# The second expert layer's first product for batches 1 to 3: seven quarter products in place of eight

## The chip, the cores and the metric

The kernel runs on one core of one Trainium2 chip. The metric is the device time of one execution in microseconds. Engines are named as the profile names them: PE is the matrix engine (its weight loads are PEld), DVE the vector engine, ACT the scalar engine, POOL the GpSimd engine, SP the engine whose queue issues the transfers here.

## The reference

Attention over q, k and v of 4 batches by 8 heads by 1152 positions of 64, with pairs of query rows averaged, gives 2304 rows x of 512 columns, 576 rows for each batch. A first expert layer maps them back to 2304 by 512. The change is in the second:

```python
def _moe2_ref(x, w1, w2, w3, w_out) -> np.ndarray:
    h = np.maximum(np.maximum(x @ w1, x @ w2), x @ w3)
    return (h @ w_out).astype(np.float32)
```

Here x is 2304 by 512, each of w1, w2 and w3 is 512 by 768, w_out is 768 by 512.

## The kernel before, in words

Every number is carried as a pair of 16-bit floats, a high part and the rest, so each 32-bit product is three matmuls: high by high, high by rest, rest by high. The kernel has three stages that run into each other: attention, the first expert layer (`up_step`, `down_step`, whose result goes to DRAM as `y_d` for each batch, L680), and the second expert layer. While the first layer finishes, `w_m_steps` (L756) loads w1 to w3, scales them and splits them into `wm` (the two parts, three matrices, four 128-row blocks `kt`, 768 columns).

The second layer goes batch by batch. `load_y(b)` (L806) makes the batch's scale, loads `yf` from `y_d` and splits it into `yh`: the high part on POOL (L825), the rest on DVE (L827). `h2_group(b, half, ff, yh)` (L847) makes one 128 by 288 block of h: for each of the three matrices, 12 matmuls of 288 columns (four `kt` by three) into one PSUM bank (L854), so 36 matmuls a group and 12 groups a batch (two halves of the rows, six blocks `ff` of the 768 columns). ACT copies the first bank to `mx` (L858), DVE takes the maximum with the second and third (L859, L860), ACT writes the high part of h (L862) and DVE the rest (L863). The six banks of `ps2` hold two groups.

`w_o_steps` (L780) loads w_out in six pieces: `to_f32` (L240 to L254) turns each from 64-bit words into 32-bit floats with one ACT and four DVE instructions (L245, L247, L248, L251, L253), then it is scaled and split (L237, L238 of `split_rows`). `out_tiles(b)` (L866) makes four 128-row tiles of the output with 18 matmuls of 512 columns each (L871), an ACT copy with the scale (L874) and a store (L876). The last 64 rows of two batches share a tile in `out_rest` (L879): 36 matmuls into the two halves of a bank (L885), two ACT copies (L889), two stores.

The order of the first two stages is written out in a table. In the second layer the tile framework orders each engine's queue: each engine's instructions stand in a fixed queue, made ahead of the run by taking, as the engine comes free in the framework's own reckoning, a ready instruction that comes early in the program. Batch 0's groups are interleaved with the pieces of `w_o_steps`; from batch 1 on the tiles of the batch before come between the groups. The pool `wrw` has three buffers under the tag `raw`; the pieces of w1 to w3 and of w_out and the `yf` tiles take turns in them.

## Time and profile before

| what | us |
|---|---|
| median of 3 runs | 1154.99 |
| lowest and highest | 1154.86, 1156.99 |
| the profiled execution's own time | 1153.67 |
| its span, from the first instruction to the last | 1151.9 |
| PE busy in the span | 1056.3 |
| DVE busy in the span | 851.4 |

The profile is of one execution on the one core. Times in rows are counted from the start of the span; between the span and the execution's own time lie 1.8 us. An instruction's own duration includes its start-up and the way of its last result, so two in a row on one engine overlap in the rows: what one costs in a full queue is read from the distance of their starts. Granted clock (PEclk) is a share of PE's full 2.4 GHz: 1.00 is that, 0.50 is 1.2 GHz.

### The profile page before, as it was taken

To read this page: it belongs to the slowest core of one execution; us is meant where nothing else is said; L and a number is where in the kernel's file an instruction comes from. 1 tells how busy PE (TensorE), PEld (TensorE's weight loads), DVE (VectorE), ACT (ScalarE), POOL (GpSimd) and SP (SyncE) were. 2 spreads that over 40 slices of the span, in tenths; PEclk is the share of its full clock that TensorE was granted. 3 is DMA by queue.
4 is the path that set the end of the run, shared out by engine and by line. 5 is a ranking of instruction groups with operands and counts; after the bars stand their busy time and mean duration, and the time that the engine had idled before them with its cause. 6 is when DMAs were issued, how large, how long until landed. Compare 5 with 4: busy or idle time off the path is not lost.

```text
span 1151.9 us, 26593 instructions
## 1 busy us (share of the span) xinstructions
PE 1056.3 (92%) x11061; PEld 870.0 (76%) x11061; DVE 851.4 (74%) x1440; ACT 737.9 (64%) x1301; POOL 149.5 (13%) x160
## 2 busy tenths in 40 slices
PE   1578988899999999999998999997799999999998
PEld 1356865778888888888887888886797877767674
DVE  6999898789989899888897888877987532422220
ACT  6688887877888878888886888875564211112111
POOL 2301011221001222111122010000200110100000
PEclk9898998899999999999999999998899999999999
DMA  9962353378667898665688656557335110000001
GB/s 330 221 199 87 101 129 83 92 160 156 117 118 143 174 176 172 129 118 118 142 170 163 116 114 105 104 91 212 115 129 164 42 40 19 11 19 20 19 19 46
DMA packets 273753, 134.90 MB, mean 117 GB/s; under 512 B 229088, under 2 KB 256736, under 8 KB 272608
## 3 DMA queue, kind: packets, MB, share of 16 engines
q1 hardware_dynamic: 273632, 133.20, 51.0%
q8 instruction: 87, 1.43, 0.5%
q14 instruction: 34, 0.28, 0.1%
HBM read 62.39 MB, written 9.44 MB: 62 GB/s over the span
## 4 chain that ended last, share of the span: by engine, by line
PE 44%; DVE 3%; DMA 1%; ACT 1%; issue 1%; SPq 0%; POOL 0%; ACTq 0%; POOLq 0%; DVEq 0%
PE p L854 18%; PE py L673 7%; PE ph L648 6%; PE po L871 5%; PE sc L472 3%; PE av L581 3%; PE tr L536 1%; PE por L885 1%; DVE t L654 1%; DMA vn<-in_v_dram 0%; DVE st_m L247 0%; DMA raw_o<-in_moe_w_out_dram 0%; DVE st_m L253 0%; DVE st_m L251 0%; DMA kn<-in_k_dram 0%
## 5 line engine op out<-in xcount | busy, mean ns | idle before, releaser
L648 PE MATMUL ph<-xh,win 128*128 128x192 f16 x2304 | 209.0, 251 | 9.7 <-POOL xh L358 7.1
L854 PE MATMUL p<-yh,wm 128*128 128x288 f16 x1728 | 214.8, 286 | 1.6 <-DVE yh L827 0.8
L487 DVE TENSOR_REDUCE st<-sc 128x1 f32<-128x1152 f32 x144 | 194.7, 1352 | 20.9 <-PE sc L472 20.3
L648 PEld LDWEIGHTS <-win 128*128 128x128 f16 x2304 | 197.8, 100 | 14.3 <-issue 9.9
L673 PE MATMUL py<-g,wou 128*128 128x192 f16 x2304 | 199.1, 247 | 6.0 <-ACT g L657 5.7
L854 PEld LDWEIGHTS <-wm 128*128 128x128 f16 x1728 | 169.0, 98 | 47.0 <-issue 2.5
L673 PEld LDWEIGHTS <-wou 128*128 128x128 f16 x2304 | 189.7, 98 | 13.8 <-issue 12.7
L494 ACT ACTIVATE pf<-sc,st,esc 128x1152 f32<-128x1152 f32 x144 | 188.6, 1310 | 14.2 <-DVE st L489 6.6
L472 PE MATMUL sc<-kst,qst 128*64 128x512 f16 (+3 forms) x1152 | 169.0, 332 | 16.8 <-DMA kst<-kpre 7.2
L472 PEld LDWEIGHTS <-qst 128*64 128x64 f16 (+1 forms) x1152 | 80.6, 105 | 77.0 <-issue 27.3
L536 PE MATMUL tr<-ident,pf 128*128 128x128 f32 x648 | 89.4, 288 | 18.1 <-ACT pf L494 17.5
L862 ACT ACTIVATE h<-mx 128x288 f16<-128x288 f32 x48 | 21.2, 442 | 128.8 <-DVE mx L860 128.8
L560 DVE TENSOR_TENSOR hl<-pf,hl 128x1152 f16<-128x1152 f32 x72 | 98.3, 1366 | 3.7 <-ACT hl L558 1.7
L859 DVE TENSOR_TENSOR mx<-p,mx 128x288 f32<-128x288 f32 x48 | 21.8, 456 | 105.1 <-PE p L854 104.6
L536 PEld LDWEIGHTS tr<-ident,pf 128*128 128x128 f32 x648 | 75.2, 148 | 27.4 <-ACT pf L494 20.7
L581 PE MATMUL av<-pt,vhl 128*64 128x192 f16 x1944 | 87.1, 247 | 0.0
L558 ACT ACTIVATE hl<-pf 128x1152 f16<-128x1152 f32 x72 | 83.5, 1160 | 1.5
L581 PEld LDWEIGHTS <-vhl 128*64 128x64 f16 x1944 | 79.3, 110 | 6.8 <-issue 6.4
L657 ACT ACTIVATE g<-t,dgs 128x384 f16<-128x384 f32 x96 | 58.0, 609 | 15.3 <-DVE t L655 14.8
L652 ACT ACTIVATE t<-ph,Uv 128x384 f32<-128x384 f32 x96 | 55.0, 574 | 15.7 <-PE ph L648 14.7
L871 PE MATMUL po<-wo,h 128*128 128x512 f16 x288 | 64.3, 379 | 0.0
L659 DVE SCALAR_TENSOR_TENSOR g<-t,dgs,g 128x384 f16<-128x384 f32 x96 | 62.0, 648 | 2.7 <-ACT g L657 2.4
(178 smaller groups left out, 1264.9 us busy)
## 6 DMA issues: line engine op xcount, KB each, us to landing
vn<-in_v_dram SPq DMA_DIRECT2D x16, 576.0 KB, 4.9
kn<-in_k_dram SPq DMA_DIRECT2D x16, 576.0 KB, 4.4
raw_m<-in_moe_w_dram SPq DMA_DIRECT2D x12, 768.0 KB, 4.3
raw_in<-in_moe_w_in_dram SPq DMA_DIRECT2D x8, 1024.0 KB, 6.6
qn<-in_q_dram SPq DMA_DIRECT2D x24, 256.0 KB, 4.0
raw_ou<-in_moe_w_out_dram SPq DMA_DIRECT2D x10, 512.0 KB, 4.1
qst<-qst SPq DMA_DIRECT2D x48, 96.0 KB, 2.5
y_d<-ys SPq DMA_DIRECT2D x48, 96.0 KB, 2.0
```

Source lines behind the costliest of these rows:

```text
L472: nc.tensor.matmul(sc[m0:m1, n0:n1], qst[b, i, p][who][:, var, m0:m1], ks[:, h, n0:n1], start=(var == 0), stop=(var == 1))
L487: nc.vector.tensor_reduce(out=m, in_=sc, axis=AX.X, op=ALU.max, negate=True)
L494: nc.scalar.activation(out=pf, in_=sc, func=AF.Exp, bias=nb, scale=e, accum_out=sums[b, i, p][:, who:who + 1])
L536: nc.tensor.transpose(tr[:, c * P:(c + 1) * P], pf[:, c * P:(c + 1) * P], ident)
L558: nc.scalar.activation(out=hl[:, 0], in_=pf, func=AF.Copy)
L560: nc.vector.tensor_tensor(out=hl[:, 1], in0=pf, in1=hl[:, 0], op=ALU.subtract)
L581: nc.tensor.matmul(acc[64 * h:64 * h + 64], vhl[b, p][:, vi, h, c, :], pt[:, h, pi * KT + c, :], start=(c == 0 and e == 0), stop=(c == KT ...
L648: nc.tensor.matmul(ph[:, a], win[:, wi, kt, ff * P:(ff + 1) * P], x[:, xi, kt], start=(kt == 0 and e == 0), stop=(kt == KD - 1 and e == 2))
L659: nc.vector.scalar_tensor_tensor(out=g[:, 1, fs, :], in0=t2, scalar=gs, in1=g[:, 0, fs, :], op0=ALU.mult, op1=ALU.subtract)
L673: nc.tensor.matmul(py, wou[:, ff // 2, wi, ff % 2, m * P:(m + 1) * P], g[:, gi, ff, :], start=(ff == 0 and e == 0), stop=(ff == NF - 1 and ...
L854: nc.tensor.matmul(ph[:, :NB2], wm[:, wi, i, kt, ff * P:(ff + 1) * P], yh[:, yi, kt, n0:n0 + NB2], start=(kt == 0 and e == 0), stop=(kt == ...
L871: nc.tensor.matmul(po, h2t[b][:, hi, ff, t * P:(t + 1) * P], wo[:, wi, ff, :], start=(ff == 0 and e == 0), stop=(ff == NF2 - 1 and e == 2))
```

## The change

For batches 1 to 3 the product of a batch's 576 rows with each of the three matrices is cut into quarters (two halves of the 512 inner columns, two halves of rows, two halves of the 768 columns) and made by Winograd's form of Strassen's scheme. `weight_sums(j)` forms three sums of weight quarters for each of three column blocks j (two additions on POOL, the rest on DVE, the split on ACT and DVE), `sum_over(j)` a fourth, written over a quarter that batch 0 needs no more (three passes on POOL, one on ACT and DVE each). `load_parts(b)` takes the place of `load_y(b)` and forms the sums of the rows (four passes on DVE, and a split into seven pairs on ACT and DVE). `unit(b, j, i)` makes the four blocks of h for one j and one matrix i with seven products of six matmuls; the sums of products are made by accumulating in a PSUM bank and by additions on DVE. Batch 0 keeps `h2_group`; `plan` says which steps follow each of its 12 groups. PE's order is now the program's. `load_y(0)` splits on ACT and DVE. Even batches keep 640 rows of h (their 576 and 64 of the next batch's), so each output tile has 128 rows; the last tile is made in two halves of 256 columns. Output tiles use the two banks of `psg`. Powers of two in the scales are changed to leave room for the sums (left out below, as is the removed code that stands in the functions above).

```diff
         for h in range(2):
-            st = ep.tile([P, 3, DM], F32, tag="wst", bufs=2, name=f"st_o{h}")
+            st = ws[:, 1 + h].rearrange("p a b c d e -> p (a b c d e)").bitcast(F32)[:, :3 * DM]
+            st = st.rearrange("p (a b) -> p a b", a=3)
...
-    def load_y(b):
+    def y_scale(b):
...
+    def load_y(b):
+        y_scale(b)
         yh = wst.tile([P, 2, KD, SQ], F16, tag="st", name=f"yh{b}")
         for k2 in range(KD // 2):
             yf = wrw.tile([P, 2, SQ], F32, tag="raw", name=f"yf{b}_{k2}")
             nc.sync.dma_start(out=yf, in_=y_d[b][:, 2 * k2:2 * k2 + 2])
             for a in range(2):
                 kt = 2 * k2 + a
-                nc.gpsimd.tensor_scalar(out=yh[:, 0, kt, :], in0=yf[:, a], scalar1=ys[:, kt:kt + 1], scalar2=1.0,
-                                        op0=ALU.mult, op1=ALU.mult)
-                nc.vector.scalar_tensor_tensor(out=yh[:, 1, kt, :], in0=yf[:, a], scalar=ys[:, kt:kt + 1],
-                                               in1=yh[:, 0, kt, :], op0=ALU.mult, op1=ALU.subtract)
+                split_rows(yh[:, 0, kt, :], yh[:, 1, kt, :], yf[:, a], ysc[b][:, kt:kt + 1])
         return yh
...
+    HM = NF2 // 2
+    def store_h2(b, ff, half, m):
+        n0 = half * NB2
+        if b % 2 == 0:
+            cuts = [(h2t[b], n0, 0, NB2)]
+        elif half == 0:
+            cuts = [(h2t[b - 1], SQ, 0, 64), (h2t[b], 0, 64, NB2)]
+        else:
+            cuts = [(h2t[b], n0 - 64, 0, NB2)]
+        for hh, d0, c0, c1 in cuts:
+            hi, lo = (hh[:, e, ff, d0:d0 + c1 - c0] for e in range(2))
+            nc.scalar.activation(out=hi, in_=m[:, c0:c1], func=AF.Copy, scale=2.0 ** -16)
+            nc.vector.scalar_tensor_tensor(out=lo, in0=m[:, c0:c1], scalar=2.0 ** -16, in1=hi, op0=ALU.mult,
+                                           op1=ALU.subtract)
     def h2_group(b, half, ff, yh):
...
+        store_h2(b, ff, half, m)
+    def quarter(e, m, k, j):
+        return wm[:, e, :, 2 * k:2 * k + 2, (j + HM * m) * P:(j + HM * m + 1) * P]
+    def pass_(eng, out_, a, b_, op):
+        eng.tensor_tensor(out=out_, in0=a, in1=b_, op=op)
+    q_ = lambda e, m, k, j: quarter(e, m - 1, k - 1, j)
+    def weight_sums(j):
+        t1 = wrw.tile([P, 2, 3, 2, P], F32, tag="raw", name=f"ws{j}")
+        t2 = wrw.tile([P, 2, 3, 2, P], F32, tag="raw", name=f"wt{j}")
+        s1, s2, s4 = t1[:, 0], t1[:, 1], t2[:, 0]
+        def parts(n, x):
+            hi, lo = ws[:, j, n, 0], ws[:, j, n, 1]
+            nc.scalar.activation(out=hi, in_=x, func=AF.Copy)
+            pass_(nc.vector, lo, x, hi, ALU.subtract)
+        pass_(nc.gpsimd, s1, q_(0, 2, 1, j), q_(0, 2, 2, j), ALU.add)
+        pass_(nc.vector, s1, s1, q_(1, 2, 1, j), ALU.add)
+        pass_(nc.vector, s1, s1, q_(1, 2, 2, j), ALU.add)
+        parts(0, s1)
+        yield
+        pass_(nc.vector, s2, s1, q_(0, 1, 1, j), ALU.subtract)
+        pass_(nc.vector, s2, s2, q_(1, 1, 1, j), ALU.subtract)
+        parts(1, s2)
+        yield
+        pass_(nc.gpsimd, s4, q_(0, 1, 2, j), s2, ALU.subtract)
+        pass_(nc.vector, s4, s4, q_(1, 1, 2, j), ALU.add)
+        parts(2, s4)
+        yield
+    def sum_over(j):
+        s3 = wrw.tile([P, 3, 2, P], F32, tag="raw", name=f"wv{j}")
+        hi, lo = quarter(0, 1, 0, j), quarter(1, 1, 0, j)
+        pass_(nc.gpsimd, s3, q_(0, 1, 1, j), hi, ALU.subtract)
+        pass_(nc.gpsimd, s3, s3, q_(1, 1, 1, j), ALU.add)
+        pass_(nc.gpsimd, s3, s3, lo, ALU.subtract)
+        nc.scalar.activation(out=hi, in_=s3, func=AF.Copy)
+        pass_(nc.vector, lo, s3, hi, ALU.subtract)
+    def load_parts(b):
+        yf = []
+        for k2 in range(2):
+            f = wrw.tile([P, 2, SQ], F32, tag="raw", name=f"yf{b}_{k2}")
+            nc.sync.dma_start(out=f, in_=y_d[b][:, 2 * k2:2 * k2 + 2])
+            yf.append(f)
+        scale_y(b)
+        yield
+        for k2 in range(2):
+            for a in range(2):
+                nc.scalar.activation(out=yf[k2][:, a], in_=yf[k2][:, a], func=AF.Copy,
+                                     scale=ysc[b][:, 2 * k2 + a:2 * k2 + a + 1])
+        rw = yp.tile([P, 3, 2, 2, NB2], F16, tag="rw", name=f"yr{b}")
+        ts = wst.tile([P, 4, 2, 2, NB2], F16, tag="st", name=f"yt{b}")
+        b11, b12 = yf[0][:, :, :NB2], yf[0][:, :, NB2:]
+        b21, b22 = yf[1][:, :, :NB2], yf[1][:, :, NB2:]
+        def parts(d, x):
+            nc.scalar.activation(out=d[:, 0], in_=x, func=AF.Copy)
+            pass_(nc.vector, d[:, 1], x, d[:, 0], ALU.subtract)
+        parts(rw[:, 0], b11)
+        yield
+        pass_(nc.vector, b11, b12, b11, ALU.subtract)
+        parts(ts[:, 0], b11)
+        yield
+        parts(rw[:, 2], b22)
+        pass_(nc.vector, b12, b22, b12, ALU.subtract)
+        yield
+        pass_(nc.vector, b22, b22, b11, ALU.subtract)
+        parts(ts[:, 1], b22)
+        yield
+        parts(rw[:, 1], b21)
+        parts(ts[:, 2], b12)
+        yield
+        pass_(nc.vector, b21, b21, b22, ALU.subtract)
+        parts(ts[:, 3], b21)
+        both_y[b] = rw, ts
+        yield
+    both_y = {}
+    def product(ps, w, x, first, last):
+        for kt in range(2):
+            for e, (wi, xi) in enumerate(((0, 0), (0, 1), (1, 0))):
+                nc.tensor.matmul(ps[:, :NB2], w(wi, kt), x[:, xi, kt], start=(first and kt == 0 and e == 0),
+                                 stop=(kt == 1 and e == 2), skip_group_check=not first)
+    tops = {}
+    def unit(b, j, i):
+        rw, ts = both_y[b]
+        raw_w = lambda m, k: lambda e, kt: wm[:, e, i, 2 * k - 2 + kt, (j + HM * m - HM) * P:(j + HM * m - HM + 1) * P]
+        sum_w = lambda n: lambda e, kt: ws[:, j, n, e, i, kt]
+        key = f"{b}_{j}_{i}"
+        bank = lambda x: ps2.tile([P, 512], F32, tag="p2", name=f"p{x}_{key}")
+        def copied(ps, tag):
+            c = ep.tile([P, NB2], F32, tag=tag, bufs=2, name=f"{tag}_{key}")
+            nc.scalar.activation(out=c, in_=ps[:, :NB2], func=AF.Copy)
+            return c
+        def block(q_, ps, other):
+            ff, half = j + HM * (q_ // 2), q_ % 2
+            if i == 0:
+                m = tops[b, j, q_] = ep.tile([P, NB2], F32, tag="mx", name=f"mx{b}_{ff}_{half}")
+                if other is None:
+                    nc.scalar.activation(out=m, in_=ps[:, :NB2], func=AF.Copy)
+                else:
+                    nc.vector.tensor_tensor(out=m, in0=ps[:, :NB2], in1=other, op=ALU.add)
+                return
+            m, x = tops[b, j, q_], ps[:, :NB2]
+            if other is not None:
+                nc.vector.tensor_tensor(out=other, in0=ps[:, :NB2], in1=other, op=ALU.add)
+                x = other
+            nc.vector.tensor_tensor(out=m, in0=x, in1=m, op=ALU.max)
+            if i == 2:
+                store_h2(b, ff, half, m)
+        a = bank("a")
+        product(a, raw_w(1, 1), rw[:, 0], True, False)
+        s1 = copied(a, "s1")
+        b_ = bank("b")
+        product(b_, sum_w(0), ts[:, 0], True, False)
+        s5 = copied(b_, "s5")
+        yield
+        product(a, sum_w(1), ts[:, 1], False, False)
+        s2 = copied(a, "s2")
+        c = bank("c")
+        product(c, raw_w(1, 2), rw[:, 1], True, True)
+        block(0, c, s1)
+        product(b_, sum_w(2), rw[:, 2], False, True)
+        block(1, b_, s2)
+        product(a, raw_w(2, 1), ts[:, 2], False, False)
+        block(3, a, s5)
+        yield
+        product(a, raw_w(2, 2), ts[:, 3], False, True)
+        block(2, a, None)
+        yield
+    def out_tile(b, t, last=False):
         hh = h2t[b]
+        r0 = b * SQ + t * P + 64 * (b % 2)
+        g = gd2["mid", b] if t == 4 else gd2[b]
+        cuts = ((0, DM // 2), (DM // 2, DM)) if last else ((0, DM),)
+        for c0, c1 in cuts:
+            po = psg.tile([P, 512], F32, tag="g1", name=f"po{b}_{t}_{c0}")[:, :c1 - c0]
+            order_ = [ff for j in range(HM) for ff in (j, j + HM)] if b else list(range(NF2))
+            for n, ff in enumerate(order_):
                 for e, (hi, wi) in enumerate(((0, 0), (0, 1), (1, 0))):
+                    nc.tensor.matmul(po, hh[:, hi, ff, t * P:(t + 1) * P], wo[:, wi, ff, c0:c1],
+                                     start=(n == 0 and e == 0), stop=(n == NF2 - 1 and e == 2))
+            os = ep.tile([P, DM], F32, tag="os", bufs=3, name=f"os{b}_{t}_{c0}")[:, :c1 - c0]
+            nc.scalar.activation(out=os, in_=po, func=AF.Copy, scale=g)
+            nc.sync.dma_start(out=out[r0:r0 + P, c0:c1], in_=os)
     dn.close()
...
+    hp = ctx.enter_context(tc.tile_pool(name="hp", bufs=2))
+    wsp = ctx.enter_context(tc.tile_pool(name="wsp", bufs=1))
+    yp = ctx.enter_context(tc.tile_pool(name="yp", bufs=2))
+    ep = ctx.enter_context(tc.tile_pool(name="ep", bufs=6))
+    ws = wsp.tile([P, HM, 3, 2, 3, 2, P], F16, name="ws")
+    room_h = lambda b: hp.tile([P, 2, NF2, SQ + 64], F16, tag="h2", name=f"h2_{b}")
+    def second():
+        out_scale(0)
+        yield from load_parts(1)
+        out_scale(1)
+    w_o, y1, sums_of = w_o_steps(), second(), [weight_sums(j) for j in range(HM)]
+    plan = {0: (w_o, 2), 1: (w_o, 2), 2: (w_o, 2), 3: (sums_of[0], 2), 4: (sums_of[0], 2), 5: (w_o, 9), 6: (y1, 4),
+            7: (y1, 9), 8: (sums_of[1], 2), 9: (sums_of[1], 2), 10: (sums_of[2], 2), 11: (sums_of[2], 2)}
+    with tc.manual_schedule(engines={mybir.EngineType.PE}):
+        h2t[0] = room_h(0)
+        for g in range(2 * NF2):
+            h2_group(0, g // NF2, g % NF2, first_h)
+            run(*plan[g])
+            if g >= NF2 + HM:
+                sum_over(g - NF2 - HM)
+        todo = [(0, t) for t in range(4)]
+        prev = None
+        for b in range(1, B):
+            h2t[b] = room_h(b)
+            slots = (1, 3, 5, 7) if len(todo) == 4 else (0, 2, 4, 6, 8)
+            nxt = load_parts(b + 1) if b + 1 < B else iter(())
+            for n, (j, i) in enumerate((j, i) for j in range(HM) for i in range(3)):
+                u = unit(b, j, i)
+                run(u, 1)
+                if prev is not None:
+                    run(prev, 1)
+                run(u, 1)
+                prev = u
+                if n >= 1:
+                    next(nxt, None)
+                if n == 8:
+                    for _ in nxt:
+                        pass
+                    if b + 1 < B:
+                        out_scale(b + 1)
+                if n in slots:
+                    out_tile(*todo.pop(0))
+            assert not todo
+            if b % 2 == 1:
+                todo = [(b - 1, 4)]
+            todo += [(b, t) for t in range(4)]
+        run(prev, 1)
+        for n, (b, t) in enumerate(todo):
+            out_tile(b, t, n == len(todo) - 1)
 _INS = ['q', 'k', 'v', 'moe_w_in', 'moe_w_out', 'moe2_w1', 'moe2_w2', 'moe2_w3', 'moe2_w_out']
```

## Rows read from the trace of the kernel before

**Rows 1.** Stretches of batches 0 to 3: PE, PEld, DVE, ACT, POOL, clock, DMA, GB/s.

```profile
862.90:884.00 21.10, 19.78 (x160) 15.52 (x160) 19.05 (x38) 9.95 (x24) 3.58 (x3) 1.00 0.57 174
884.00:917.70 33.70, 33.70 (x280) 27.01 (x278) 20.06 (x43) 10.88 (x20) 3.90 (x4) 1.00 0.18 54
917.70:1127.50 209.80, 209.80 (x1555) 150.16 (x1553) 58.24 (x126) 40.31 (x86) 7.79 (x8) 1.00 0.07 23
```

**Rows 2.** Timeline of PE in the second layer (start, length, instructions merged).

```profile
908.88 13.39 PE L854 MATMUL p<-yh,wm 128*128 128x288 f16 x108
...
1050.17 17.81 PE L854 MATMUL p<-yh,wm 128*128 128x288 f16 x144
1067.82 4.05 PE L871 MATMUL po<-wo,h 128*128 128x512 f16 x18
1071.71 8.98 PE L854 MATMUL p<-yh,wm 128*128 128x288 f16 x72
...
1143.10 4.08 PE L885 MATMUL por<-wo,h 128*64 128x512 f16 x36
```

**Rows 3.** Timeline of ACT at the end.

```profile
1147.26 1.39 ACT L889 ACTIVATE osr<-por,gk 64x512 f32<-64x512 f32 x2 [3.32 <-PE por L885]
```

**Rows 4.** Timeline of DVE, instructions of 768 columns.

```profile
808.80 0.95 DVE L253 SCALAR_TENSOR_TENSOR st_m<-raw_m,st_m 128x768 uint32<-128x768 uint32 x1
809.67 0.95 DVE L251 SCALAR_TENSOR_TENSOR st_m<-raw_m,st_m 128x768 uint32<-128x768 uint32 x1
```

**Rows 5.** Timeline of DVE in batch 0 of the second layer.

```profile
873.35 0.82 DVE L859 TENSOR_TENSOR mx<-p,mx 128x288 f32<-128x288 f32 x2
...
884.29 0.69 DVE L253 SCALAR_TENSOR_TENSOR st_o<-raw_o,st_o 128x512 uint32<-128x512 uint32 x1
...
895.95 0.15 DVE L176 TENSOR_SCALAR U_o<-sum_o 128x1 uint32<-128x1 uint32 x1
...
898.13 3.55 DVE L238 SCALAR_TENSOR_TENSOR wo<-st_o,s_o,wo 128x1536 f16<-128x1536 f32 x2 [1.13 <-ACT wo L237]
```

**Rows 6.** One tile's instructions, yh on DVE (min, median, max ns; first, last start).

```profile
L827 DVE SCALAR_TENSOR_TENSOR yh<-yf,ysc,yh x16: 802/1212/1295, 862.8 to 997.5; 128x576 f16<-128x576 f32 x16
```

**Rows 7.** Groups of POOL instructions (count, busy us, mean ns, idle before).

```profile
L433 POOL TENSOR_TENSOR qn<-qn 128x384 f32<-128x384 f32 x24 | 28.8, 1201 | 109.6 <-DMA qn<-in_q_dram 82.3 <-DVE st L489 7.1 <-DVE xf L595 6.8
...
L775 POOL TENSOR_TENSOR wm<-st_m,wm 128x2304 f16<-128x2304 f32 x1 | 4.7, 4728 | 0.1
```

**Rows 8.** Timeline of DVE around three POOL instructions.

```profile
286.62 2.19 DVE L560 TENSOR_TENSOR hl<-pf,hl 128x1152 f16<-128x1152 f32 x1
...
378.66 1.36 DVE L546 TENSOR_TENSOR pt<-tr,pt 128x1152 f16<-128x1152 f32 x1
...
404.85 1.36 DVE L560 TENSOR_TENSOR hl<-pf,hl 128x1152 f16<-128x1152 f32 x1
```

**Rows 9.** Timeline of POOL in the same three places.

```profile
286.59 1.00 POOL L433 TENSOR_TENSOR qn<-qn 128x384 f32<-128x384 f32 x1 [0.32 <-DMA qn<-in_q_dram]
...
378.32 1.23 POOL L358 TENSOR_SCALAR kpre<-kn,sb 128x1152 f16<-128x1152 f32 x1 [0.26 <-DVE sqq L176]
...
405.09 1.57 POOL L358 TENSOR_SCALAR qpre<-qn,sqq 128x384 f16<-128x384 f32 x1 [3.87 <-ACT ys L677]
```

**Rows 10.** Timeline of DVE while batch 1's rows are split.

```profile
912.66 0.44 DVE L859 TENSOR_TENSOR mx<-p,mx 128x288 f32<-128x288 f32 x1
913.02 2.14 DVE L827 SCALAR_TENSOR_TENSOR yh<-yf,ysc,yh 128x576 f16<-128x576 f32 x2
915.09 0.45 DVE L860 TENSOR_TENSOR mx<-p,mx 128x288 f32<-128x288 f32 x1
```

**Rows 11.** Stretches around a gap on PE, columns as in rows 1.

```profile
816.00:820.00 4.00, 0.00 (x0) 0.00 (x0) 4.00 (x5) 0.54 (x2) 1.40 (x1) 0.83 0.18 33
820.00:824.00 4.00, 3.88 (x25) 3.56 (x25) 2.54 (x6) 2.82 (x5) 0.00 (x0) 0.50 0.73 236
824.00:828.00 4.00, 4.00 (x42) 3.88 (x41) 3.65 (x9) 4.00 (x8) 0.00 (x0) 0.81 0.40 155
```

More of the change, by code (lines that the diff above doesn't have):

```diff
@@ L813, in load_y @@
         nc.vector.tensor_reduce(out=zs, in_=z, axis=AX.XY, op=ALU.add)
[L814 removed]
+        root_scale(hu, c, all_add(zs, 1, f"y{b}"), 1, 4.0)
         hus[b] = hu
[L817 to L818 removed]
+        ysc[b] = late.tile([P, KD], F32, tag="ys", name=f"ysc{b}")
+        nc.vector.tensor_scalar(out=ysc[b], in0=u_m, scalar1=c, scalar2=None, op0=ALU.mult)
+    def load_y(b):
+        y_scale(b)
         yh = wst.tile([P, 2, KD, SQ], F16, tag="st", name=f"yh{b}")
@@ L879, in out_rest @@
-    def out_rest(b0):
-        os = ep.tile([P, DM], F32, tag="os", bufs=3, name=f"osr{b0}")
-        po = ps2.tile([P, 512], F32, tag="p2", name=f"por{b0}")
-        for ff in range(NF2):
-            for e, (hi, wi) in enumerate(((0, 0), (0, 1), (1, 0))):
-                for j in range(2):
-                    nc.tensor.matmul(po[64 * j:64 * j + 64, :], h2t[b0 + j][:, hi, ff, 4 * P:SQ], wo[:, wi, ff, :],
-                                     start=(ff == 0 and e == 0), stop=(ff == NF2 - 1 and e == 2))
-        for j in range(2):
-            rows = slice(64 * j, 64 * j + 64)
-            nc.scalar.activation(out=os[rows], in_=po[rows], func=AF.Copy, scale=gd2[b0 + j][rows])
-            r0 = (b0 + j) * SQ + 4 * P
-            nc.sync.dma_start(out=out[r0:r0 + 64, :], in_=os[rows])
-        yield
@@ L894, in body @@
-    nxt = first_y[0]
-    dn.close()
-    hp = ctx.enter_context(tc.tile_pool(name="hp", bufs=3))
-    ep = ctx.enter_context(tc.tile_pool(name="ep", bufs=3))
-    wgen = w_o_steps()
-    pend = None
-    for b in range(B):
-        yh = nxt
-        h2t[b] = hp.tile([P, 2, NF2, SQ], F16, tag="h2", name=f"h2_{b}")
-        for half in range(2):
-            for ff in range(NF2):
-                h2_group(b, half, ff, yh)
-                if b == 0:
-                    next(wgen, None)
-                    if half == 1 and ff == 3:
-                        run(wgen)
-                        out_scale(0)
-                        nxt = load_y(1)
-                        out_scale(1)
-                elif b + 1 < B and half == 0 and ff == 0:
-                    nxt = load_y(b + 1)
-                    out_scale(b + 1)
-                if pend is not None and ff % 2 == 1:
-                    if next(pend, "end") == "end":
-                        pend = None
-        if pend is not None:
-            run(pend)
-        if b % 2 == 0:
-            pend = out_tiles(b)
-        else:
-            def both(b=b):
-                yield from out_tiles(b)
-                yield from out_rest(b - 1)
-            pend = both()
```

36 lines of the change are left out of this document (14 added, 22 removed).

## The prediction

> **What bounds the kernel now.** I read the busy time by stretches first. From 884.0 to 1127.5 us PE is busy in every microsecond at full clock [rows 1]; DVE is busy 20.06 of 33.70 us in the second half of batch 0 and 58.24 of 209.80 us in batches 1 to 3. So in batches 1 to 3 a matmul that goes takes its whole spacing off the time, and DVE has room for more; in batch 0 DVE has some 13 us left, and it is there that most of the new preparation is put. The timeline of PE then gives the spacing [rows 2], that of DVE the prices of its instructions [rows 4 to 6], POOL's groups those of its own [rows 7], and a pair of timelines what the two do to each other [rows 8, 9].
>
> **What PE loses.** A unit has seven products of six matmuls, 42, where eight would have 48. There are 3 batches by 3 column blocks by 3 matrices, 27 units: 162 matmuls fewer. 144 of them take from 1050.17 to 1067.82 [rows 2], 0.1226 us each: **19.9 us off**. A tile of 18 takes 3.89 us (1067.82 to 1071.71), a tile of `out_rest`, 4.08 recorded against 4.05, the same; 18 before, 18 after: nothing. At the end two copies of 0.69 us stand in a row behind the last matmul [rows 3]; after it one of 256 columns: between 0.7 (a copy as long as now) and 1.0 (half as long) goes, I take **0.9 off**.
>
> **What the added instructions cost.** On DVE one over 768 columns costs 0.87 us, the distance of two starts [rows 4]; one over 288 costs 0.37 (two in 0.82, the second 0.45 long) [rows 5]; one over 576 takes 0.80 undisturbed [rows 6], less 0.08 of overlap 0.72; a half of w_out's split 1.77, a scale instruction 0.15 [rows 5]. An addition over 768 columns on POOL is a third of the 4.73 us of the one over 2304, 1.58 us; by the other group, 1.20 for 384, it would be 2.40 [rows 7]. I take the first, which has 16-bit operands too.
>
> The Trainium skill says on VectorE: DVE Perf Modes, in Terms, that a flush follows each DVE operation and the next can't issue before the pipe is empty. So read, whole durations would add up, 0.95 and 0.46 in place of 0.87 and 0.37: some 4.7 us more for the 67 instructions of the queue below, and a sum of 1.4 off where I get 6.1. The rows show the starts closer than the durations, and my sum goes by them.
>
> **DVE's queue up to the first need.** Until 885.0, when the last piece of w_out is converted [rows 5], the three raw buffers are held by those pieces and little is added. From there I count what stands in the program before the third block of batch 1's first unit, for whose reading the seventh product's bank waits. Groups 4 to 11 of batch 0: 24 by 0.37, 8.9. `weight_sums` 0 and 1: 16 by 0.87, 13.9. The first `sum_over`: 0.9. w_out's split: 3.5. `load_parts(1)`: seven splits and four differences, 11 by 0.72, 7.9. Ten scale instructions: 1.5. Three blocks: 1.1. Together 37.7, to 922.7. PE ends batch 0 at 917.7 (908.88 and 72 by 0.1226) [rows 2] and can make eight products of 0.735 us before that seventh one: to 923.6. By DVE alone nothing waits, with 0.9 us to spare.
>
> But POOL adds too. A DVE instruction with two SBUF operands that starts beside a POOL addition takes 2.19 us where it takes 1.36, and POOL's 1.57 beside such a one; one that reads PSUM takes its 1.36 beside POOL [rows 8, 9]. So POOL's time adds to DVE's but for what DVE reads from PSUM, some fifth of this queue (19 by 0.37). Seven additions belong to it (two for each sum, three for `sum_over`), the first before 885: 6 by 1.58 by 0.8, 7.6 us. The third block is then read at 930.3 and PE **waits 6.7 us**. Ends: 0, if POOL's additions fall where DVE has nothing to do, and 14 at the dearer price with nothing beside it.
>
> What is left, sum 2 (7.0), two `sum_over` (1.7) and eight additions on POOL (10.1 as above), 18.8 us, isn't needed before the seventh unit. Six units and three tiles give PE 42.6 us (6 by 42 by 0.1226, 3 by 3.89); DVE's own work in them is 42 by 0.37, 15.5, and seven instructions of `load_parts(2)`, 5.0: with the rest 39.3. It fits, but only just, and instructions stand in line behind each other: I take **4 us**, between 0 and the whole 18.8.
>
> **Smaller terms.** After a gap of some 5 us on PE the granted clock was 0.50, which is 1.2 GHz, for a stretch of 4 us with PE busy, then 0.81 [rows 11]; a like gap costs up to 2.5 us, none costs nothing: with waits in pieces **1.0**. In a unit without an output tile behind it, two products of the next (1.47 us) cover the reading of the third block, which with a backlog of one long instruction is about what DVE needs: 14 units by 0.1, **1.5**; ends 0 and 14 by 0.7. The last unit has no such cover: four DVE instructions, **1.5**. `load_y(0)` trades POOL's part for one on ACT of like length: 0, within 1 either way. Transfers: two loads a batch as before, stores one fewer; SP and the DMA engines, at 0.07 of their time [rows 1], hide them, and without that cover one load late by its landing would be seen once a batch. The sum over partitions in `load_parts` now has a fixed place on PE; its operands hang on nothing new: 0, or a microsecond behind a full DVE queue.
>
> **Sum.** 19.9 and 0.9 off, 6.7, 4.0, 1.0, 1.5 and 1.5 on: 6.1 off the profiled execution's 1153.67 (span 1151.9 and 1.8 around it), 1147.6. The median of the runs lies 1.3 above that execution: **1149**.
>
> **Rivals.** *First, the preparation goes ahead of the units.* DVE's queue is made by program order among what is ready: batch 1's second and third split went before an older group's maximum, whose operands were there [rows 10]. If sum 2's first addition is reckoned to end before the first block stands ready (917.7 and four products, 920.6), the whole sum 2 (7.0 and 2.5 of POOL) and the second `sum_over` (0.9 and 3.8) go ahead of the units' blocks: 14.2 more, the rest 1. The wait is 21.9, the gap long enough for the full 2.5 of clock: 6.6 on, 1161.6 on the median's scale, slower. For it speak the order in [rows 10] and that `plan` puts both sums before batch 1; against it that sum 2 needs a raw buffer which `load_parts(1)` and sum 1 hold until late. The Trainium skill's page SBUF — State Buffer, Who interferes with whom, has the blocking as a rule (two SBUF inputs against a POOL instruction that reads SBUF: the second waits out the first); the trace agrees, 2.19 against 1.36.
>
> *Second, it hides.* DVE alone is done at 922.7, before 923.6; if POOL's additions fall beside PSUM reads or into waits for ACT, no wait is left: 20.8 off, 1.0 for units, 1.0 for the end, 18.8 off, 1136.2. Against it: there are 15 additions, 23.7 us of POOL's time, in a stretch that DVE fills.
>
> *Third, the removal isn't had*, since each unit without a tile waits for its third block: a microsecond in 14 units, 12.5 more than I took, 1161.4. It decides if DVE's order puts row sums between a unit's blocks. Against it DVE's 28% in batches 1 to 3, which becomes about half (63 by 0.37 and 7.9 in some 63 us a batch).
>
> **How the numbers follow.** My forecast has a chance of 0.42, with a range of its own of 1143 to 1155; the first rival 0.27, the second 0.25, the third 0.06. 0.2%, 2.3 us, is about what a measurement of this kernel can tell from no change. Faster by more: 0.36 of my case, the whole second, 0.01 of the first: 0.62. Within: 0.05, 0.05 and 0.01: 0.11. Slower: 0.27. The range reaches over the second rival's middle to the first's, 1135 to 1162; a fifth, the far ends of both, is left out.
>
> **What would show it.** Batches 1 to 3 should have 1134 matmuls of 288 columns, at the same 0.1226 where PE is full. PE should be full through batch 0 to near 917 and then show a gap of some 7 us in pieces, ended by DVE, before the first output tile; DVE should be full from 885 to 930, with instructions over 768 columns of up to 2.4 us beside POOL's. A gap of 20 us with sum 2's instructions in it means the first rival; no gap, the second; short waits for DVE in every other unit to the end, the third. I am wrong in the ground if the spacing is longer in units than in groups, or if PE waits already within batch 0.

## The result, and the profile after

The change makes the kernel slower: ratio to the kernel before 1.0058, with a 95% interval of 1.0039 to 1.0077.

| | before | after |
| --- | --- | --- |
| median of 5 runs each, side by side | 1156.09 us | 1162.23 us |
| lowest, highest | 1154.86, 1157.18 | 1161.14, 1165.31 |
| profiled execution (span) | 1153.67 (1151.9) | 1161.14 (1159.4) |
| first product of the second layer | 862.87 | 864.79 |
| batch 0, to the first unit (before: to batch 1) | 54.83 | 56.67 |
| batches 1 to 3, to the last row of tiles | 209.76 | 214.93 |
| last tiles to the end of the span | 24.4 | 23.0 |

Of the 7.5 us between the spans, 1.9 are there before the second layer begins, in a stage that the change does not touch. Over all profiled executions of this study, one for each kernel, that start lies between 862.87 and 868.05 us. So beside the ratios I compare the **second layer's length**, from its first product to the end of the span: 289.0 before, 294.6 after.

The busy time by stretches of the changed kernel answers to [rows 1]; columns are PE, PEld, DVE, ACT, POOL, granted clock, DMA, GB/s.

```profile
862.00:884.00 22.00, 20.44 (x159) 15.59 (x157) 17.55 (x38) 12.79 (x29) 1.64 (x1) 0.92 0.45 138
884.00:918.00 34.00, 34.00 (x281) 27.26 (x280) 30.07 (x59) 18.34 (x32) 3.44 (x2) 1.00 0.12 36
918.00:950.00 32.00, 15.91 (x90) 10.23 (x88) 30.96 (x31) 10.29 (x20) 22.92 (x11) 0.68 0.06 18
950.00:1127.00 177.00, 174.74 (x1256) 122.59 (x1254) 92.36 (x220) 68.90 (x160) 3.08 (x2) 1.00 0.08 29
```

The loss is in the third row: around the first unit PE is busy in half of the time, at a clock of 0.68, while DVE is full with only 31 instructions, one a microsecond. PE's timeline there (start, length, then tiles and, behind the x, the matmuls merged; in brackets the idle time before and its releaser):

```profile
921.46 0.90 PE L979 MATMUL pa<-yr,wm 128*128 128x288 f16 x6
922.19 0.90 PE L979 MATMUL pb<-yt,ws 128*128 128x288 f16 x6
929.47 1.60 PE L979 MATMUL pa<-yt,ws 128*128 128x288 f16 x6 [6.38 <-ACT s L993]
930.86 1.64 PE L979 MATMUL pc<-yr,wm 128*128 128x288 f16 x6
932.30 1.09 PE L979 MATMUL pb<-yr,ws 128*128 128x288 f16 x6
939.01 0.66 PE L979 MATMUL pa<-yt,wm 128*128 128x288 f16 x2 [5.62 <-ACT wm L930]
943.76 1.14 PE L979 MATMUL pa<-yt,wm 128*128 128x288 f16 x4 [4.09 <-DVE wm L894]
944.70 1.64 PE L979 MATMUL pa<-yr,wm 128*128 128x288 f16 x6
...
950.12 0.90 PE L979 MATMUL pc<-yr,wm 128*128 128x288 f16 x6
950.86 0.90 PE L979 MATMUL pb<-yr,ws 128*128 128x288 f16 x6
```

Batches 1 to 3 hold 27 units of 42 matmuls at 0.1226 us and 13 tiles of 3.89, 189.6 us; they take 214.93. Of the **25.3 lost**, PE's waits are 19.3 (16.1 in the three above, the rest in four waits under a microsecond), and 6.0 is left. Most of that are matmuls at a spacing of 1.44 for six in place of 0.735: from 921.46 to 950.12, where the clock is back, ten products of six take 28.66 us, less the waits 12.6, in place of 7.35, which is 5.2 more. The rest is small and spread. The three waits are for a copy of a bank by ACT (s1), and for the two halves of the overwritten quarter of column block 0, which `sum_over(0)` makes. ACT's timeline shows why the copy, of a bank that PE had finished before 923, comes at 929:

```profile
923.76 0.43 ACT L870 ACTIVATE h<-mx 128x288 f16<-128x288 f32 x1
928.27 0.84 ACT L906 ACTIVATE ws<-wt 128x768 f16<-128x768 f32 x1 [4.08 <-DVE wt L894]
929.02 0.39 ACT L993 ACTIVATE s<-pa 128x288 f32<-128x288 f32 x1
```

ACT is idle for 4.08 us with the bank ready. Its instructions start in the order of its queue, and the split in front of the copy, a part of weight sum 1 that nobody needs before the fourth unit, waits for DVE. DVE's timeline and then POOL's show what DVE does:

```profile
923.42 3.95 DVE L894 TENSOR_TENSOR yt<-yf,yt 128x576 f16<-128x576 f32 x2
927.29 0.95 DVE L894 TENSOR_TENSOR wt<-wt,wm 128x768 f32<-128x768 f32 x1
928.16 1.89 DVE L871 SCALAR_TENSOR_TENSOR h<-mx,h 128x288 f16<-128x288 f32 x1
...
934.96 2.38 DVE L894 TENSOR_TENSOR ws<-ws,wm 128x768 f32<-128x768 f32 x1
937.27 0.45 DVE L1003 TENSOR_TENSOR mx<-pc,s 128x288 f32<-128x288 f32 x1
937.63 0.44 DVE L1003 TENSOR_TENSOR mx<-pb,s 128x288 f32<-128x288 f32 x1
938.00 1.66 DVE L894 TENSOR_TENSOR ws<-ws,wm 128x768 f32<-128x768 f32 x1
...
944.94 0.46 DVE L1003 TENSOR_TENSOR mx<-pa,s 128x288 f32<-128x288 f32 x1 [0.23 <-PE pa L979]
```

```profile
891.98 1.66 POOL L894 TENSOR_TENSOR wt<-wm,ws 128x768 f32<-128x768 f16 x1 [9.79 <-DVE ws L894]
...
922.55 2.10 POOL L894 TENSOR_TENSOR wt<-wm,ws 128x768 f32<-128x768 f16 x1 [22.76 <-DVE yt L894]
924.73 2.03 POOL L894 TENSOR_TENSOR wv<-wm 128x768 f32<-128x768 f16 x1
...
934.68 6.47 POOL L894 TENSOR_TENSOR wv<-wv,wm 128x768 f32<-128x768 f32 x3
```

Three things are to be seen. The order: behind 932 all `ws` instructions of DVE belong to sum 2, two of its additions stand before the first unit's first two blocks, and four additions and two splits before the third (944.94). The prices: beside POOL an instruction with two SBUF operands takes up to 1.89 or 2.38 us where alone it takes 0.45 or 0.95; the blocks at 937, which read PSUM, keep their 0.45. From 922 to 954 what they are longer by adds up to 12.9 us over POOL's twelve additions there, 1.07 each. And POOL itself stood idle for 22.76 us, until `load_parts(1)` gave back the raw buffers that `sum_over(0)` and sum 1's last part needed; then all its additions came at once, beside the fullest stretch of DVE.

The end has one short copy in place of [rows 3]: the last copy ends 0.56 us behind PE, where it ended 1.47 behind.

```profile
1136.39 19.63 PE L1044 MATMUL po<-wo,h 128*128 128x512 f16 x108
```

```profile
1156.11 0.47 ACT L1047 ACTIVATE os<-po,gk 128x256 f32<-128x256 f32 x1 [1.49 <-PE po L1044]
```

### The profile page after: what moved, and what is told of

The parts are those of the page before. It is cut to its first block, busy times and chain, and to the rows that moved or that the text cites. A ratio compares the mean times of both kernels' runs of the same rounds, so it can differ in the third digit from the quotient of the medians.

```text
span 1159.4 us, 26453 instructions
## 1 busy us (share of the span) xinstructions
PE 1043.8 (90%) x10881; PEld 860.4 (74%) x10881; DVE 928.6 (80%) x1585; ACT 788.9 (68%) x1415; POOL 163.9 (14%) x159
## 4 chain that ended last, share of the span: by engine, by line
PE 39%; DVE 7%; ACT 2%; DMA 1%; issue 1%; SPq 1%; POOL 0%; ACTq 0%; DVEq 0%; POOLq 0%
PE py L674 7%; PE ph L649 6%; PE pa L979 6%; PE po L1044 6%; PE p L881 4%; PE sc L473 3%; PE pb L979 3%; PE av L582 3%; PE pc L979 1%; PE tr L537 1%; DVE ws L894 1%; ACT yf L944 1%; DMA raw_m<-in_moe_w_dram 1%; DVE t L655 1%; DVE yt L894 0%
## 5 line engine op out<-in xcount | busy, mean ns | idle before, releaser
L674 PEld LDWEIGHTS <-wou 128*128 128x128 f16 x2304 | 190.9, 99 | 14.7 <-issue 13.4
L537 PE MATMUL tr<-ident,pf 128*128 128x128 f32 x648 | 90.2, 290 | 18.2 <-ACT pf L495 17.7
L979 PEld LDWEIGHTS <-wm 128*128 128x128 f16 x648 | 64.2, 100 | 33.1 <-ACT wm L930 5.9
L1044 PE MATMUL po<-wo,h 128*128 128x512 f16 (+1 forms) x342 | 72.3, 368 | 0.0
L653 ACT ACTIVATE t<-ph,Uv 128x384 f32<-128x384 f32 x96 | 55.0, 574 | 14.7 <-PE ph L649 13.5
L509 POOL COPY rb<-sm 128x128 f32<-128x128 f32 x48 | 20.5, 428 | 314.0 <-DVE sm L506 117.1
L979 PEld LDWEIGHTS <-ws 128*128 128x128 f16 x486 | 48.4, 100 | 20.8 <-issue 7.6
L656 DVE SCALAR_TENSOR_TENSOR t<-t 128x384 f32<-128x384 f32 x96 | 59.7, 622 | 3.1
```

The costliest lines, as they stand in the source:

```text
L537: nc.tensor.transpose(tr[:, c * P:(c + 1) * P], pf[:, c * P:(c + 1) * P], ident)
L674: nc.tensor.matmul(py, wou[:, ff // 2, wi, ff % 2, m * P:(m + 1) * P], g[:, gi, ff, :], start=(ff == 0 and e == 0), stop=(ff == NF - 1 and ...
L979: nc.tensor.matmul(ps[:, :NB2], w(wi, kt), x[:, xi, kt], start=(first and kt == 0 and e == 0), stop=(kt == 1 and e == 2), skip_group_check ...
L1044: nc.tensor.matmul(po, hh[:, hi, ff, t * P:(t + 1) * P], wo[:, wi, ff, c0:c1], start=(n == 0 and e == 0), stop=(n == NF2 - 1 and e == 2))
```

## The experiments

Theory: the time is lost because preparation that is needed later (sums 1 and 2, the overwritten quarters) stands ahead of the first unit's work in the queues of DVE and ACT, and POOL's share of it holds DVE up. Rivals: it is only the raw buffers that hold `sum_over(0)`; it is the clock; the units themselves are slow. All runs, with the time beside runs of the kernel before on the same chip:

| run | median us | ratio (95%) | second layer us |
| --- | --- | --- | --- |
| the changed kernel | 1162.23 | 1.0058 (1.0039 to 1.0077) | 294.6 |
| own buffer | 1160.47 | 1.0037 (1.0021 to 1.0052) | 293.5 |
| late sums | 1156.69 | 1.0016 (0.9994 to 1.0037) | 290.3 |
| tiles first | 1156.06 | 1.0001 (0.9988 to 1.0014) | 290.1 |
| no POOL | 1152.44 | 0.9961 (0.9948 to 0.9973) | 285.8 |
| one sum (work left out) | 1145.53 | 0.9921 (0.9909 to 0.9934) | 276.9 |
| no POOL, late, early quarter | 1146.26 | 0.9932 (0.9917 to 0.9947) | 278.8 |
| no POOL, late, tiles | 1147.61 | 0.9941 (0.9929 to 0.9954) | 280.3 |
| no POOL, tiles | 1144.70 | 0.9912 (0.9898 to 0.9926) | 279.5 |
| no POOL, early quarter, tiles | 1144.04 | 0.9893 (0.9867 to 0.9919) | 277.3 |
| no POOL, late, early quarter, one tile | 1146.67 | 0.9918 (0.9894 to 0.9943) | 278.7 |
| waits filled | 1169.26 | 1.0118 (1.0099 to 1.0137) | 303.2 |
| POOL kept, early quarter, tiles | 1153.19 | 0.9973 (0.9956 to 0.9989) | 286.7 |

**Own buffer.** The overwritten quarters get two buffers that nothing else holds (the line that makes the pool `vp` is left out).

```diff
-        s3 = wrw.tile([P, 3, 2, P], F32, tag="raw", name=f"wv{j}")
+        s3 = vp.tile([P, 3, 2, P], F32, tag="wv", name=f"wv{j}")
```

> sum_over's tile gets a pool of its own (two buffers) in place of the three raw buffers, nothing else. If the raw buffers are what keeps the first sum_over late (POOL idle 22.8 us until load_parts frees one, then 5.6 and 4.1 us of PE waiting for its two writes), those two waits go and the time falls by 8 to 12 us from 1162, to 1150 to 1154. If the order of the queues alone is the cause (sums 1 and 2 ahead of the first unit's copies and blocks), the 6.4 us wait for ACT's copy stays and most of the rest turns into a wait for DVE: within 4 us of 1162.

Measured: 1160.47. The two waits for `sum_over(0)` are gone, and little is gained: batches 1 to 3 lose 19.0 us in place of 25.3, but batch 0 takes 61.93 in place of 56.67. POOL's and PE's timelines of this run:

```profile
871.46 8.15 POOL L894 TENSOR_TENSOR wv<-wv,wm 128x768 f32<-128x768 f32 x4
```

```profile
939.47 0.40 PE L979 MATMUL pa<-yt,ws 128*128 128x288 f16 x1 [6.63 <-ACT s L993]
```

The freed additions now run beside the splits of batch 0's rows, where PE waits over a microsecond for each of four, and the wait for ACT's copy stays (here behind a split of batch 1's rows that waits 5.57 us for DVE). The buffers are not the cause by themselves.

**Late sums.** Sums 1 and 2 and their quarters are issued among the first four units.

```diff
-            7: (y1, 9), 8: (sums_of[1], 2), 9: (sums_of[1], 2), 10: (sums_of[2], 2), 11: (sums_of[2], 2)}
+            7: (y1, 9)}
...
+                if b == 1 and n < 2:
+                    run(sums_of[1], 2)
+                    if n == 1:
+                        sum_over(1)
+                if b == 1 and 2 <= n < 4:
+                    run(sums_of[2], 2)
+                    if n == 3:
+                        sum_over(2)
```

> weight_sums 1 and 2 and sum_over 1 and 2 move from batch 0's last groups behind the first four units of batch 1; load_parts(2) starts three units later. If they stand ahead of the first unit in the queues, PE's 16 us of waiting and some 5 us at half clock go but for sum_over(0): 1144 to 1149. If DVE and POOL are simply short of time up to the seventh unit, the waits move into the units: 1155 to 1162. If the raw buffers are the cause, the first sum_over still waits for load_parts(1): no more than 6 us gained.

Measured: 1156.69. The long waits at the first unit become shorter ones, of 0.43 to 3.54 us, and one of 5.02 us, for a copy of ACT, comes in the third unit:

```profile
954.06 1.60 PE L979 MATMUL pa<-yt,wm 128*128 128x288 f16 x6 [5.02 <-ACT s L993]
```

The order matters (batches 1 to 3 lose 18.9 in place of 25.3), but a later place for the sums moves a part of the waiting to later units.

**Tiles first.** Two output tiles of batch 0 go ahead of the first unit.

```diff
+            if b == 1:
+                out_tile(*todo.pop(0))
+                out_tile(*todo.pop(0))
+                slots = (3, 7)
```

> Two of batch 0's four output tiles (7.8 us of matmuls) go ahead of batch 1's first unit. All theories have PE idle there for DVE and ACT, so the tiles fill a wait: 7.8 us off, and up to 3 more if the shorter gap spares the half clock: 1151 to 1155. If instead PE's work is what DVE waits for (the blocks come later, and the preparation isn't in the way), nothing is gained: 1160 to 1164.

Measured: 1156.06, between the two outcomes of the expectation: 6.2 less than the changed kernel, in the second layer 4.5 less, for 7.8 us of tiles. Nearly all waiting is now one wait:

```profile
944.72 1.60 PE L979 MATMUL pa<-yt,ws 128*128 128x288 f16 x6 [14.50 <-ACT s L993]
```

The tiles lie beside DVE's preparation but do not move its end: the third product starts at 944.72, where it started at 929.47, since ACT's copy now stands behind two splits of sum 2 as well.

**No POOL.** The same additions, on DVE.

```diff
-        pass_(nc.gpsimd, s1, q_(0, 2, 1, j), q_(0, 2, 2, j), ALU.add)
+        pass_(nc.vector, s1, q_(0, 2, 1, j), q_(0, 2, 2, j), ALU.add)
...
```

> All 15 additions of POOL go to DVE (0.87 us each there, 13 us more in its queue; POOL spends 32 us on them now). If the two engines block each other so that POOL's time counts as DVE's, DVE's queue gets shorter by 8 to 15 us and the time falls to 1148 to 1156. If they work side by side, DVE has 13 us more ahead of the units, and the time rises to 1168 to 1175.

Measured: 1152.44, 9.8 below the changed kernel and below the kernel before. The stretch of the first unit, and the groups of one addition on DVE between 884 and 960 (count, busy us, mean ns, idle before):

```profile
918.00:950.00 32.00, 20.68 (x136) 13.73 (x135) 32.00 (x49) 11.62 (x23) 0.00 (x0) 0.84 0.08 21
```

```profile
L894 DVE TENSOR_TENSOR ws<-ws,wm 128x768 f32<-128x768 f32 x12 | 11.4, 951 | 0.0
```

DVE does 49 instructions in the 32 us in which it did 31, and no addition is held: 0.951 each. **POOL gave no relief at all.** Over the whole second layer, first the changed kernel's, then this run's, DVE is busy for 2.6 us less, with fifteen additions more:

```profile
864.79:1159.40 294.61, 270.79 (x1916) 189.65 (x1915) 175.19 (x353) 116.36 (x250) 31.09 (x15) 0.96 0.12 39
866.32:1152.10 285.78, 266.71 (x1916) 187.80 (x1915) 172.57 (x368) 116.31 (x250) 0.00 (x0) 0.98 0.13 40
```

So an addition on POOL held DVE for 1.0 us on average (15 by 0.87 and 2.6, over 15) and for 1.43 at most (2.38 less 0.95); on DVE it takes 0.87. DVE's time is thus worth 2.6 of the 8.8 us by which the second layer is shorter. A fall of the clock in batch 0 that this execution does not have is 1.5 more. The rest comes with another order: here ACT makes the first unit's copies ahead of the split of sum 1, which stood in front of them in the changed kernel, so the first long wait shrinks from 6.38 to 1.36 us. ACT's timeline of this run:

```profile
924.03 0.39 ACT L993 ACTIVATE s<-pa 128x288 f32<-128x288 f32 x1
924.33 0.40 ACT L993 ACTIVATE s<-pb 128x288 f32<-128x288 f32 x1
927.29 0.84 ACT L906 ACTIVATE ws<-wt 128x768 f16<-128x768 f32 x1 [2.56 <-DVE wt L894]
```

The framework made this order anew when the additions changed engine; no run changes ACT's order alone, so what it is worth by itself stays open. One long wait was left, for `sum_over(0)`:

```profile
934.86 0.66 PE L979 MATMUL pa<-yt,wm 128*128 128x288 f16 x2 [8.02 <-ACT wm L930]
```

**One sum.** A bound from the other side, with work left out: sums and overwritten quarter are made for column block 0 alone (the steps of sums 1 and 2 also go from `plan`).

```diff
-        sum_w = lambda n: lambda e, kt: ws[:, j, n, e, i, kt]
+        sum_w = lambda n: lambda e, kt: ws[:, 0, n, e, i, kt]
...
-            if g >= NF2 + HM:
-                sum_over(g - NF2 - HM)
+            if g == NF2 + HM:
+                sum_over(0)
...
```

> The three weight sums and the overwritten quarter are made for j = 0 alone, and all units read the sums of j = 0: the sums 1 and 2 and the overwritten quarters 1 and 2 are left out. If the preparation that stands ahead of the units is what the change lost (waits of 16 us and the half clock behind them, of 25 us against an undisturbed run of units), the first unit then meets DVE and ACT queues that hold only its own preparation: waits of PE under 4 us between 921 and 950, no or one short drop of the clock, and a time of 1138 to 1146 us, 16 to 24 below the changed kernel. If the units themselves are slow (their products, block additions or bank releases), it stays above 1155.

Measured: 1145.53; in the second layer 17.7 us less than the changed kernel. One wait over a microsecond is left in it, and with it 207 matmuls run between 918 and 950 where there were 90:

```profile
927.75 0.90 PE L979 MATMUL pa<-yt,ws 128*128 128x288 f16 x6 [2.22 <-ACT s L993]
```

```profile
918.00:950.00 32.00, 28.94 (x207) 20.65 (x205) 20.34 (x45) 15.99 (x33) 0.00 (x0) 0.95 0.21 65
```

Batches 1 to 3 lose 7.2 us in place of 25.3. So the units are about as fast as the prediction's sum has them, and most of what was lost is the preparation of column blocks 1 and 2. How much of that is its place in the queues and how much DVE's time for it, this run does not tell.

**Combinations with all preparation on DVE.** "Early quarter" takes batch 0's second half in another order, so that `sum_over(0)` can be made three groups sooner:

```diff
-            h2_group(0, g // NF2, g % NF2, first_h)
+            h2_group(0, g // NF2, (g + HM * (g // NF2)) % NF2, first_h)
...
+            if g == NF2:
+                sum_over(0)
```

> Nothing is left out. All preparation on DVE, sums 1 and 2 and their overwritten quarters issued among the first four units of batch 1, and the second half of batch 0 takes its weight blocks in the order 3, 4, 5, 0, 1, 2, so that the overwritten quarter of j = 0 can be made three groups sooner. If the time is lost to DVE's queue ahead of the first unit, the wait of 8.0 us for the overwritten quarter that was left with all preparation on DVE goes, and the time is 1136 to 1143 us. If DVE's total work up to the seventh unit is what bounds (as with the late sums alone), a wait of 4 to 8 us comes back at the fourth unit and the time is 1144 to 1152.

> Nothing is left out. All preparation on DVE, late sums as in the earlier run, and two output tiles of batch 0 ahead of the first unit, which give DVE 7.7 us more before its results are wanted. If queue order and DVE's time are the whole loss: no wait of PE over 2 us in batch 1, clock 1.00 throughout, 1136 to 1142 us. If the tiles only shift the wait (their place in batch 1 is then missing as cover for the fourth unit): 1144 to 1152.

> Nothing is left out. All preparation on DVE, two output tiles of batch 0 ahead of the first unit, the sums where the changed kernel has them. All preparation on DVE alone left one wait of 8.0 us and some 5 of short ones with a short drop of the clock; the two tiles give 7.7 us of cover. If covers add up: 1143 to 1147 us. If the planner then puts still more of the sums ahead of the units' blocks: 1149 to 1154.

Measured: 1146.26, 1147.61 and 1144.70, all faster than the kernel before. The first two fall into the worse of their two bands, but not as those had it: the longest wait is still at the first unit's third product, 2.49 and 4.09 us for ACT's copy, and at the third and fourth unit there are only waits of 0.98 in the first, 0.78 and 1.60 in the second, for DVE. The third falls into its better one; the intervals of the first and the third overlap. The effects of tiles and POOL nearly add up: 0.57% and 0.97% off the changed kernel's ratio alone, 1.46% together. In the third, the one long wait is again ACT's queue, here behind the copy of an overwritten quarter. Its timelines of PE and ACT:

```profile
933.31 1.60 PE L979 MATMUL pa<-yt,ws 128*128 128x288 f16 x6 [4.12 <-ACT s L993]
```

```profile
931.54 0.84 ACT L930 ACTIVATE wm<-wv 128x768 f16<-128x768 f32 x1 [2.82 <-DVE wv L894]
932.29 0.67 ACT L1047 ACTIVATE os<-po,gk 128x512 f32<-128x512 f32 x1
932.86 0.40 ACT L993 ACTIVATE s<-pa 128x288 f32<-128x288 f32 x1
```

> Nothing is left out. All preparation on DVE, two output tiles of batch 0 ahead of the first unit, and the second half of batch 0 takes its weight blocks in the order 3, 4, 5, 0, 1, 2, with the overwritten quarter of j = 0 made right behind the first of these. With the same tiles and without this order, one wait of 4.1 us was left, for a copy of the first unit that stood in ACT's queue behind the overwritten quarter's copy, and a short drop of the clock behind it. If that queue order is the cause: the wait goes, 1139 to 1143 us. If DVE's time is what bounds, the wait only changes its name: 1144 to 1147.

> Nothing is left out. As the run with late sums, early overwritten quarter and all preparation on DVE (1146.3 us), with one output tile of batch 0 ahead of the first unit. The tile is 3.9 us long and the waits at the first unit there were 2.7 us: if covers add up, 1142 to 1145 us; if DVE is behind through the seventh unit, the same as without the tile, 1145 to 1148.

Measured: 1144.04 and 1146.67. The first loses the wait of 4.12, as the queue order has it, but others of 2.09 and 1.90 come in its place, and the time is at the edge of the band in which DVE bounds; its interval overlaps that of the run without the early quarter. The second is in the band without gain. DVE is full in all versions that make every sum on it, busy for 31.4 of the 32 us from 918 to 950 or more; here the first of the two:

```profile
918.00:950.00 32.00, 27.03 (x190) 18.28 (x189) 32.00 (x51) 15.12 (x29) 0.00 (x0) 1.00 0.11 36
```

**Waits filled.** Products that nobody reads, in the long waits of the changed kernel, to keep the clock up.

```diff
+    def filler(n, x):
+        pf = psg.tile([P, 512], F32, tag="g1", name=f"fill{n}")
+        for k in range(n):
+            nc.tensor.matmul(pf[:, :NB2], wm[:, 0, 0, 0, :P], x, start=(k == 0), stop=(k == n - 1))
...
+            filler(48, ts[:, 0, 0, 0])
...
+            filler(66, ts[:, 0, 0, 0])
```

> The changed kernel with 114 products more, whose results nobody reads, put into TensorE's two long waits of the first unit: 48 (5.9 us) ahead of the second sum's product and 66 (8.1 us) ahead of the sixth product, so that the engine is hardly idle. If the half clock behind the waits cost its 5.3 us by itself, the granted clock stays at 1.00 and the time falls to 1156 to 1159 us. If DVE and ACT set the pace there and a faster TensorE only waits for them later, the clock stays up and the time stays at 1160 to 1164; if the added products push the copies of the first unit further back in the planner's order, over 1164.

Measured: 1169.26, the third outcome. The clock stays up to 938, and then two other waits come:

```profile
934.00:938.00 4.00, 4.00 (x35) 3.19 (x34) 3.96 (x2) 1.58 (x2) 3.92 (x3) 1.00 0.02 4
938.00:942.00 4.00, 1.46 (x12) 1.03 (x11) 4.00 (x4) 0.40 (x1) 1.88 (x1) 0.95 0.00 0
942.00:946.00 4.00, 3.21 (x14) 2.05 (x14) 3.96 (x6) 1.47 (x3) 3.41 (x2) 0.50 0.00 0
```

```profile
954.15 1.60 PE L979 MATMUL pa<-yt,wm 128*128 128x288 f16 x6 [6.88 <-DVE mx L1008]
```

The fillers also changed the order that the framework made: the first unit's second copy stood ahead of sum 2's splits (931.65) and now stands behind two of them (942.35). So the run does not price the clock alone; with the clock at 1.00 through the first wait, nothing was gained here.

**POOL kept.** The fastest order, with the additions on POOL again (fifteen; the expectation's twelve is a miscount).

> Nothing is left out. The fastest version so far (two output tiles ahead of the first unit, overwritten quarter of j = 0 early; 1144.0 us with all preparation on DVE) with the twelve additions back on POOL, as the change has them. If POOL's additions hold up DVE by about their own excess (9.8 us between the changed kernel and the same without POOL), this is 1151 to 1156 us, at best level with the kernel before. If with the order repaired POOL's work lies beside other work and only relieves DVE of eleven us, it is faster than without POOL, 1136 to 1143.

Measured: 1153.19, and one long wait for ACT's copy is back:

```profile
942.92 1.60 PE L979 MATMUL pa<-yt,ws 128*128 128x288 f16 x6 [9.61 <-ACT s L993]
```

So the repaired order alone brings the change just below the kernel before (0.9973), and taking POOL's additions away brings nine more. Again this is not POOL's holding of DVE alone: DVE's busy time over the second layer is 174.72 us here and 172.21 without POOL, 2.5 apart, and ACT's copy (942.46) stands behind two splits of sum 2 and a copy of a quarter, where without POOL it came ahead of them (933.14).

## Why the prediction was wrong

**The step that failed** is "DVE's queue up to the first need", in what it left out of that queue. It counted sums 0 and 1 and put the rest (sum 2, two quarters, eight additions on POOL) behind the first unit, at 4.0 us. In the run two of sum 2's three parts stand ahead of the third block, which comes at 944.9, not 930.3. Of the 14.6 us between, sum 2's six instructions are 5.2 (6 by 0.87); POOL held DVE for 10.2 us in ten additions, not 7.6 in six; and for 4.3 DVE was idle, 3.2 of it waiting for ACT, for which the working had no term. Waits and clock together, with the terms for the units, were put at 14.7 us; they came to 25.3.

That is the **first rival**, which I held for less likely: 24.4 for wait and clock, with the 3.0 for the units 27.4, and 1161.6. The run with one sum, which leaves out this preparation, takes away 17.7 us and ends within the band of my forecast. Against the rival I had held that sum 2 needs a raw buffer that is held until late. The buffer was late indeed, but that delayed `sum_over(0)` as much, which the first unit needs: the argument cut the other way.

**That the rival's time, 1161.6, lies so near the measured 1162.23 is in part luck.** Its 27.4 is 2.1 more than was lost, and 3.8 us that it had at nothing lie ahead of the first unit (1.92 before the second layer, 1.84 in batch 0). It also saw one wait, for DVE's third block at the seventh product. The trace has three and none there: the first is at the third product, for a copy of ACT that stood behind a split, and two at the sixth, for the overwritten quarter. My working follows DVE's and POOL's queues only; ACT's queue, in which the units' copies stand in line with splits that wait for DVE, has no term in it. A copy of ACT ended the longest wait in ten of the twelve runs besides the changed kernel, and in the changed kernel itself.

**POOL's price.** The addition undisturbed was nearly right (1.58 worked out, 1.64 to 1.79 in the first three). The holding of DVE was foreseen in kind (2.19 against 1.36 in [rows 8]) and a little too dear in size, 1.26 for each addition (1.58 by 0.8) against 1.0 measured; wrong was the number of additions ahead of the third block. And I never asked what the additions would cost on DVE, 0.87. The Trainium skill's page SBUF — State Buffer, Who interferes with whom, says that a DVE instruction with two SBUF inputs contends with a GpSimd instruction that reads SBUF, and calls the contention an exclusive lock; the 2.38 against 0.951 agrees, and the PSUM-reading blocks with their 0.45 beside POOL, too. The Trainium skill's page Perfetto Trace Analysis, Optimizing Scalar/DVE Operations, says that moving work between these two engines might not help, as they share a port; DVE's busy time agrees, 175.19 us with the additions on POOL and 172.57 with them on DVE.

**The clock.** I took 1.0, with 2.5 as the upper bound from one gap. Between 929 and 950 most products ran at 1.2 GHz (a granted clock of 0.50 to 0.53 in most slices of 4 us with PE busy), and by spacing they lost 5.2. Whether they cost that by themselves is open: in the run with filled waits the clock held longer and nothing was gained, but the order changed too, and the two fastest versions, one with a short fall to 0.71 and one at 1.00 throughout, end within each other's interval.

**Right**: the removal (the units run at 0.735 us for six products, 0.1226 each, from 950 to the end; the third rival, waits in every unit, is out: behind 966 two waits under a microsecond are left); the prices of DVE's instructions by the distance of starts (0.87 and 0.37), against a sum of whole durations; the end (0.9 by the last copy). `load_y(0)` was put at 0 within 1: batch 0 took 1.84 longer, of which 1.6 is a fall of the clock to 0.59 behind the first waits in this execution. The runs without POOL, with the same waits, don't have it, nor do three of those with POOL (tiles first, one sum, waits filled).

The second rival's 1136.2, all hidden, was not reached: the fastest version still waits 8 us.

## What to carry to other kernels

When a change takes work off a full engine and pays with preparation on others, write out every in-order queue that the first consumer passes through, the copying engine's too, with the work that is only needed later: what an automatic order puts ahead of the first need decides, beside the total. A change to one engine's work can make the automatic order put another engine's queue differently, so look at that before a gain is put down to the engine. Two tiles of unrelated work ahead of the first consumer, one sum made sooner and no additions on POOL turned this change from 0.6% slower to 1.1% faster (what the earlier sum adds to the other two is not clear of noise). Before an addition goes to POOL to relieve DVE, compare what it adds to the DVE instructions beside it (here 1.0 us on average, 1.43 at most) with what it costs on DVE (0.87).
